# Attention and a feed-forward block on one core: whole chunks in kv, weight splits on VectorE alone, and queries times kv in quarters of the array

## The chip, the core and the metric

The kernel runs on one core of a Trainium2 chip. A core has TensorE (matmuls, PE in the profile, with its weight loads as PEld), VectorE (DVE), ScalarE (ACT), GpSimd (POOL) and SyncE (SP), whose queue issues most DMAs. Each engine runs its own instructions in order and waits on semaphores for the others. The scheduler that builds the program fixes the order on every engine beforehand. The metric is the device time of one execution in microseconds.

## What is computed

Linear attention over 8 batches of 8 heads, 576 positions and 64 features, followed by a feed-forward block on all 4608 tokens of 512 features:

```python
q_s = softmax(q, axis=-1); k_s = softmax(k, axis=positions)
kv  = einsum('bhsd,bhse->bhde', k_s, v)
x   = einsum('bhsd,bhde->bhse', q_s, kv)      # reshaped to (4608, 512)
h = x @ w_in                                  # 512 x 2048
g = h * clip(h + 3, 0, 6) / 6
out = g @ w_out                               # 2048 x 512
```

The weights arrive as float64 and are passed on bit for bit.

## The kernel before

Tokens are taken in three blocks of 512 and then three large blocks of 1024. In code the blocks are `j` = 0, 1, 2 and the large blocks are `s` = 0, 1, 2. Heads are handled in four pairs `hp`, so that 128 partitions hold two heads of 64 features.

**Decode.** The weights come in 16 chunks `f`, each 128 rows of w_in (turned) and of w_out. `decode` (line 127) turns the float64 bits of a chunk into float32 with four operations on VectorE (lines 134, 136, 141 and 145) and two on ScalarE (133, 144), then calls `split` (line 118): a rounded high part on ScalarE (line 120) and the rest, by a subtraction (line 121). For odd `f` above 1, seven chunks, that subtraction runs on GpSimd, otherwise on VectorE. The decode of chunk f + 2 is issued within the first block, between its matmuls for chunk f.

**kv.** `kv_of` (line 187) multiplies softmaxed keys `ke` with values `vt` over the 576 positions of one batch. Positions come in five chunks of 128, of which the last holds 64. Each chunk makes two matmuls of 64 columns, one for each head of the pair, into the upper and lower half of one bank `pkv`. The last chunk uses 64 rows. A column of ones in `vt` gives the softmax sum. The result, scaled and masked, is a block-diagonal 128x128 tile `kv` with one 64x64 block for each head. For the first two batches `ke` is made by transposing on TensorE (`k_softmax`, line 236), which fills only 64 rows of its last chunk. For the others the keys come padded.

**Queries.** `px` is `kv` times the softmaxed, turned queries `qT`. In `token_attention` (used for the third block by `block_attention` and for the large blocks by `sb_attention`) it is computed 512 tokens at a time: one matmul with all 128 rows and columns for each batch that the 512 tokens cross, in one of the two banks that `bank_a` hands out. `put` then copies the bank away: for large blocks one ScalarE copy of 128x512 into `x32` (line 377). The next unit's key maxima are turned by two transposes `pm`, which use the same two banks.

**Order.** From the second block on, TensorE's instructions keep the order in which the code is written (`ordered`, line 77). Attention for the next block is written in steps between the feed-forward matmuls of the present one: `ph` (x times w_in) and `po` (times w_out) in the blocks, and in the large blocks `x`, `y`, `z` of a scheme with seven products per pair of chunks, in `phase1` and `phase2`. So the large blocks' px come in three groups of four units: within block j = 2 for s = 0, within phase 1 of s = 0 for s = 1, and within phase 1 of s = 1 for s = 2. In the first block the scheduler alone sets TensorE's order. On the other engines it always does.

Of the kernel before, what the change touches and what calls it, by code (L numbers as in the profile page):

```python
# [1 line left out]

# [1 line left out]

# [6 lines left out]
F32 = mybir.dt.float32  # L11
# [7 lines left out]
P = 128  # L19
TB = 512  # L20
QD = 32
NC4 = TB // P
# [10 lines left out]
def attention_moe(  # L33
# [15 lines left out]
    nc = tc.nc  # L49

    B, NP, _, S = kT.shape
    D = q.shape[5]
# [7 lines left out]
    NCH = S // P + 1  # L60
    TAIL = S % P
# [14 lines left out]
    def bank_a(name):  # L76
        return ps_a.tile([P, TB], F32, name=name, tag="pa")
# [3 lines left out]
    def ordered(ins):  # L81
        if in_order:
            tc.keep_in_program_order(ins)

    def mm(out, lhsT, rhs, start, stop, goes_on=False):
        ordered(
            nc.tensor.matmul(  # L87
                out, lhsT, rhs, start=start, stop=stop, skip_group_check=goes_on
            )
        )  # L90

    def flip(out, in_):
        ordered(nc.tensor.transpose(out, in_, ident))
# [13 lines left out]
    def place(f, dt, name):  # L107
        return wp.tile([P, 4 * DM], dt, name=name, tag=f"w{f}")
# [7 lines left out]
    FROM_DRAM = 3  # L116
    whole = dr.tile([P, NFC, 2 * DM], F32, name="whole")

    def split(hi, lo, src, engine=nc.vector):
        nc.scalar.copy(hi, src)  # L120
        engine.tensor_sub(lo, src, hi.bitcast(F32))  # L121

    def load_w(f):
        raws[f] = place(f, U32, f"raw_{f}")
# [2 lines left out]
    def decode(f):  # L127

        n = 2 * DM
        pairs = raws.pop(f).rearrange("p (n two) -> p n two", two=2)  # L130
        low, high = pairs[:, :, 0], pairs[:, :, 1]
        m = moe.tile([P, n], F32, name="m", bufs=1)
        nc.scalar.activation(m, high.bitcast(F32), AF.Abs)
        nc.vector.tensor_scalar(m, m, W_MIN, W_MAX, op0=ALU.max, op1=ALU.min)
        m = m.bitcast(U32)
        nc.vector.tensor_scalar(
            m, m, 3, 0x3FFFFFFF, op0=ALU.logical_shift_left, op1=ALU.bitwise_and
        )
        v = moe.tile([P, n], F32, name="v", bufs=3)
        vu = v.bitcast(U32)  # L140
        nc.vector.scalar_tensor_tensor(  # L141
            vu, high, 0xC0000000, m, op0=ALU.bitwise_and, op1=ALU.bitwise_or
        )
        nc.scalar.activation(low, low, AF.Copy, scale=2.0**-29)
        nc.vector.tensor_tensor(vu, vu, low, op=ALU.add)
        if f // 2 >= FROM_DRAM:
            nc.sync.dma_start(whole[:, f], v)
        parts = place(f, F32R, f"w_{f}").rearrange("p (s i n) -> p s i n", s=2, i=2)
        split(
            parts[:, :, 0],  # L150
            parts[:, :, 1],
            v.rearrange("p (s n) -> p s n", s=2),
            nc.gpsimd if f % 2 and f > 1 else nc.vector,
        )
        wi[f], wo[f] = parts[:, 0], parts[:, 1]

# [2 lines left out]
    def x_block(j):  # L159
        if j not in x_tiles:  # L160
            t = xp.tile([P, 2, NCC, TB], F32R, name=f"x{j}", tag="xa")
            x_tiles[j] = t[:, 0], t[:, 1]
        return x_tiles[j]

    kvs = {}
# [22 lines left out]
    def kv_of(j, hp, ke, vt):  # L188
        pkv = bank_a("pkv")
        for c in range(NCH):  # L190
            r = slice(0, P if c < NC4 else TAIL)
            for h in range(2):
                hs = slice(h * D, (h + 1) * D)
                mm(pkv[hs, 0 : D + 1], ke[r, c, hs], vt[r, c, h, :], c == 0, c == NCH - 1)
        rk = att.tile([P, 1], F32, name="rk", bufs=2)
        nc.vector.tensor_scalar_add(rk, pkv[:, D : D + 1], EPS)
        nc.vector.reciprocal(rk, rk)
        kv = att.tile([P, P], F32, name="kv", bufs=10)
        nc.vector.scalar_tensor_tensor(
            kv.rearrange("p (h d) -> p h d", h=2),  # L200
            pkv[:, 0:D].rearrange("p (o d) -> p o d", o=1).broadcast_to([P, 2, D]),
            rk,
            mask.rearrange("p (h d) -> p h d", h=2),
            op0=ALU.mult,
            op1=ALU.mult,
        )
        kvs[j, hp] = kv
# [29 lines left out]
    def k_softmax(j, km, ke, kt):  # L237
        nc.vector.tensor_reduce(km, kt, axis=AX.X, op=ALU.max, negate=True)
        nc.scalar.activation(kt, kt, AF.Exp, bias=km)
        yield  # L240
        a = bank_a if j else bank
        pe, pe2 = a("pe"), a("pe2")
        for c in range(NC4):
            flip(pe[:, c * P : (c + 1) * P], kt[:, c * P : (c + 1) * P])
        flip(pe2[0:TAIL, 0:P], kt[:, TB:S])
        nc.scalar.copy(ke[:, 0:NC4].rearrange("p c n -> p (c n)"), pe)
        nc.scalar.copy(ke[0:TAIL, NC4], pe2[0:TAIL, 0:P])

    def attention(j, hp):

        if not j:
            kt, qt, qT, vt, ke = first[hp]
        else:
            kt, ke, vt = load_k(j, hp)
            qt = att.tile([P, TB], F32, name="qt", bufs=1)
            nc.sync.dma_start(qt, q[j, hp])
            qt = qt.rearrange("p (c h d) -> p c h d", c=NC4, h=2)
        km = att.tile([P, 1], F32, name="km", bufs=2)
        ks = k_softmax(j, km, ke, kt)
        next(ks)  # L260
        q_softmax(qt, j > 0, nc.vector if j else nc.gpsimd)
        yield
        next(ks, None)
        tp = (bank_a if j else bank)("tp")
        for c in range(NC4):
            flip(tp[:, c * P : (c + 1) * P], qt[:, c].rearrange("p h d -> p (h d)"))
        if j:
            qT = att.tile([P, TB], F32, name="qT")
        nc.scalar.copy(qT, tp)
        yield  # L270
        kv_of(j, hp, ke, vt)
        yield
        px = (bank_a if j else bank)("px")
        e = SHIFT * j
        for b, lo, hi in ((j - 1, 0, e), (j, e, TB)):
            if lo < hi:
                mm(px[:, lo:hi], kvs[b, hp], qT[:, lo:hi], True, True)
        x_hi, x_lo = x_block(j)
        split(x_hi[:, hp, :], x_lo[:, hp, :], px)

    def load_k(b, hp, tokens=False):
# [45 lines left out]
    def x_of(s):  # L327

        if "x" not in held:
            held["x"] = xp.tile([P, NCC, SB], F32, name="x32", tag="xa")  # L330
        return held["x"]

    def token_attention(t0, n, hp, put):

        need = [b for b in range(t0 // S, (t0 + n - 1) // S + 1)]
        qt = att.tile([P, SB], F32, name="qt", bufs=1)[:, 0:n]
        at = (t0 - TURNED) // TB
        nc.sync.dma_start(
            qt.rearrange("p (b n) -> p b n", n=TB),
            qf[at : at + n // TB, hp].rearrange("b p n -> p b n"),  # L340
        )
        loads = {b: load_k(b, hp, tokens=True) for b in need if (b, hp) not in kvs}
        yield
        new = {}
        for b, (kt, ke, vt) in loads.items():
            km = att.tile([P, 1], F32, name="km", bufs=2)
            nc.vector.tensor_reduce(km, kt, axis=AX.X, op=ALU.max)  # L347
            kb = att.tile([P, P], F32, name="kb", bufs=2)
            nc.gpsimd.tensor_copy(kb, km.broadcast_to([P, P]))
            new[b] = ke, vt, kb  # L350
        qT = q_softmax_t(qt)
        yield
        for ke, vt, kb in new.values():
            pm = bank_a("pm")
            flip(pm[:, 0:P], kb)
            nc.vector.tensor_sub(
                ke, ke, pm[:, 0:P].rearrange("p (o n) -> p o n", o=1).broadcast_to([P, NCH, P])
            )
            nc.scalar.activation(ke, ke, AF.Exp)
        yield  # L360
        yield
        for b, (ke, vt, kb) in new.items():
            kv_of(b, hp, ke, vt)
        yield
        for c in range(n // TB):
            px = bank_a("px")
            at = t0 + c * TB
            for b in need:
                lo, hi = max(b * S - at, 0), min((b + 1) * S - at, TB)
                if lo < hi:  # L370
                    mm(px[:, lo:hi], kvs[b, hp], qT[:, c * TB + lo : c * TB + hi], True, True)
            put(c, hp, px)
        yield

    def sb_attention(s):
        def put(c, hp, px):
            nc.scalar.copy(x_of(s)[:, hp, c * TB : (c + 1) * TB], px)

        return [token_attention(START + s * SB, SB, hp, put) for hp in (0, 2, 1, 3)]

    def block_attention(j):
        def put(c, hp, px):
            x_hi, x_lo = x_block(j)
            split(x_hi[:, hp, :], x_lo[:, hp, :], px)

        return [token_attention(j * TB, TB, hp, put) for hp in range(NP)]
# [492 lines left out]
```

## Time and profile before

| | us |
|---|---|
| median of 3 runs (range) | 863.46 (861.28 to 864.54) |
| the profiled execution | 863.42 |
| its span in the profile | 861.6 |
| TensorE busy | 816.8 |
| VectorE busy | 683.7 |
| ScalarE busy | 443.6 |
| GpSimd busy | 80.1 |

The profile records one execution. "Busy" sums the time in which an engine had at least one instruction running. Matmuls are pipelined, so TensorE's busy time is not a measure of how well it is used. A row of the groups gives line, engine, operation, tiles (written <- read), shape and count, then busy time, mean of one in ns, and the idle time of the engine just before with the releasers. A row of the timeline gives start, length, engine and operation. The chain is the series of steps, each released by the one before, that ends with the last instruction.

### The profile page before, as it was taken

Reading aid. Unit: us, or ns where it says so; the run is one execution under the profiler, and the core shown is the slowest. Engines: PE = TensorE matmul, PEld = TensorE weight load, DVE = VectorE, ACT = ScalarE, POOL = GpSimd, SP = SyncE. Lnnn points to the kernel's source line nnn. Section 1 sums busy time; section 2 is a strip of 40 time slices with the busy share of each in tenths; the row PEclk is TensorE's granted clock in tenths of the full one; section 3 lists DMA queues with packets and bytes.
Section 4 is the critical chain, followed back from the end, with each engine's and each line's share of the span. In section 5 each row is a group of like instructions: output and inputs, shape, how many; then the busy total and the mean of one; then the engine's idle time right before and its main releaser. Section 6 shows DMA issues by size and latency. Waiting matters only on the chain.

```text
span 861.6 us, 11761 instructions
## 1 busy us (share of the span) xinstructions
PE 816.8 (95%) x4032; PEld 654.0 (76%) x4032; DVE 683.7 (79%) x1088; ACT 443.6 (51%) x717; POOL 80.1 (9%) x178
## 2 busy tenths in 40 slices
PE   4689998999999998999999999999999999999997
PEld 3468786877887876887877777777788788887886
DVE  7998998998778988578998985688597845648763
ACT  7886673443344444345555553544555534445543
POOL 5111212110100110001102000011000000000000
PEclk9789999999999999999999999999999999999999
DMA  9997667578549660578875667775566776666672
GB/s 366 413 407 265 210 201 233 198 243 279 169 150 366 213 240 25 169 259 272 271 256 167 194 205 238 225 229 168 172 178 193 236 231 195 193 193 191 193 234 88
DMA packets 75643, 192.30 MB, mean 223 GB/s; under 512 B 7232, under 2 KB 19520, under 8 KB 73536
## 3 DMA queue, kind: packets, MB, share of 16 engines
q1 hardware_dynamic: 75008, 190.51, 67.3%
q10 hardware_dynamic: 576, 1.05, 0.3%
q8 instruction: 32, 0.52, 0.2%
q14 instruction: 27, 0.22, 0.1%
HBM read 147.49 MB, written 44.04 MB: 222 GB/s over the span
## 4 chain that ended last, share of the span: by engine, by line
PE 67%; DVE 18%; DMA 5%; issue 4%; ACT 3%; POOL 1%; SPq 0%; ACTq 0%; DVEq 0%; POOLq 0%
PE x L87 24%; PE po L87 12%; PE ph L87 10%; PE y L87 9%; PE z L87 9%; DMA kt<-in_kT_dram 2%; DVE g L515 2%; PE px L87 2%; PE pkv L87 2%; DVE gp L121 1%; DVE gf L121 1%; DVE v L141 1%; DVE right L121 1%; DVE km L347 1%; DMA wf<-gp 1%
## 5 line engine op out<-in xcount | busy, mean ns | idle before, releaser
L120 ACT CAST gf<-g 128x512 fp32r<-128x512 f32 x168 | 103.9, 622 | 96.3 <-DVE gf L121 48.0
L87 PE MATMUL ph<-x,w 128*128 128x512 f32 x576 | 147.9, 405 | 4.4 <-POOL w L121 2.0
L87 PE MATMUL po<-w,gp 128*128 128x512 f32 x576 | 146.9, 404 | 3.5 <-DVE gp L121 2.2
L121 DVE TENSOR_TENSOR gf<-g,gf 128x512 fp32r<-128x512 f32 x168 | 112.9, 686 | 31.8 <-ACT gf L120 31.0
L87 PEld LDWEIGHTS ph<-x,w 128*128 128x128 f32 x576 | 111.7, 195 | 31.5 <-POOL w L121 2.9
L87 PEld LDWEIGHTS po<-w,gp 128*128 128x128 f32 x576 | 108.4, 192 | 29.4 <-DVE gp L121 3.3
L87 PE MATMUL x<-right,gp 128*128 128x512 f32 x384 | 95.0, 392 | 2.9 <-DVE g L555 2.9
L87 PE MATMUL x<-gf,gp 128*128 128x512 f32 x384 | 89.0, 389 | 0.0
L87 PEld LDWEIGHTS x<-right,gp 128*128 128x128 f32 x384 | 71.6, 188 | 19.2 <-DVE g L555 3.7
L87 PEld LDWEIGHTS x<-gf,gp 128*128 128x128 f32 x384 | 72.1, 188 | 15.0
L514 ACT ACTIVATE g<-ph,three 128x512 f32<-128x512 f32 x48 | 32.8, 686 | 64.6 <-PE ph L87 64.6
L120 ACT CAST gp<-g 128x512 fp32r<-128x512 f32 x48 | 29.6, 620 | 39.8 <-DVE g L515 39.7
L514 ACT ACTIVATE v<-g,three 128x1024 f32<-128x1024 f32 x24 | 27.6, 1151 | 42.4 <-DVE g L559 42.4
L87 PE MATMUL x<-right,left 128*128 128x512 f32 x192 | 47.8, 392 | 0.8 <-DVE g L555 0.8
L87 PE MATMUL y<-right,gp 128*128 128x512 f32 x192 | 48.2, 395 | 0.0
L87 PE MATMUL x<-gf,left 128*128 128x512 f32 x192 | 46.1, 392 | 0.9 <-DVE gf L121 0.9
L87 PE MATMUL z<-gf,gp 128*128 128x512 f32 x192 | 45.7, 392 | 1.0 <-DVE gf L121 0.9
L87 PEld LDWEIGHTS z<-gf,gp 128*128 128x128 f32 x192 | 35.7, 188 | 10.1 <-DVE gf L121 2.7
L87 PEld LDWEIGHTS x<-gf,left 128*128 128x128 f32 x192 | 35.7, 188 | 10.1 <-DVE gf L121 2.8
L87 PEld LDWEIGHTS x<-right,left 128*128 128x128 f32 x192 | 35.7, 188 | 8.6 <-DVE g L555 1.3
L87 PEld LDWEIGHTS y<-right,gp 128*128 128x128 f32 x192 | 35.6, 188 | 8.0 <-issue 0.5
L514 ACT ACTIVATE g<-g,three 128x512 f32<-128x512 f32 x24 | 17.4, 725 | 39.5 <-DVE g L548 39.5
(135 smaller groups left out, 1324.6 us busy)
## 6 DMA issues: line engine op xcount, KB each, us to landing
gp<-wf SPq DMA_DIRECT2D x112, 512.0 KB, 3.6
left<-wf SPq DMA_DIRECT2D x56, 512.0 KB, 3.7
raw<-in_w_dram SPq DMA_DIRECT2D x16, 1024.0 KB, 14.2
wf<-gp SPq DMA_DIRECT2D x64, 256.0 KB, 3.6
wf<-w SPq DMA_DIRECT2D x48, 256.0 KB, 3.9
vt<-in_v_dram SPq DMA_DIRECT2D x28, 325.0 KB, 5.4
kt<-in_kT_dram SPq DMA_DIRECT2D x28, 288.0 KB, 3.5
ke<-in_k_dram SPq DMA_DIRECT2D x24, 320.0 KB, 4.7
```

The source lines that it names most:

```text
L87: nc.tensor.matmul(out, lhsT, rhs, start=start, stop=stop, skip_group_check=goes_on)
L120: nc.scalar.copy(hi, src)
L121: engine.tensor_sub(lo, src, hi.bitcast(F32))
L141: nc.vector.scalar_tensor_tensor(vu, high, 0xC0000000, m, op0=ALU.bitwise_and, op1=ALU.bitwise_or)
L347: nc.vector.tensor_reduce(km, kt, axis=AX.X, op=ALU.max)
L514: nc.scalar.activation(r, h, AF.Relu, bias=three, scale=1.0)
L515: nc.vector.scalar_tensor_tensor(g, r, 6.0, h, op0=ALU.min, op1=ALU.mult)
```

## The change

Three parts.

1. `split` no longer takes an engine: all subtractions of the decode run on VectorE.
2. `kv_of` uses 128 rows in every chunk. The rows that have no positions are filled with zeros by GpSimd where `ke` comes from transposes.
3. `token_attention` hands the queries to `put`, which issues the matmuls. For large blocks these are 64x64 quarters: the two heads are the two halves of the rows, and the two runs of 512 tokens are the two halves of the columns. Each head has a bank, and each run of tokens half of its partitions. The four results are copied with four ScalarE copies of 64x512. The third block keeps whole matmuls.

```diff
-    def split(hi, lo, src, engine=nc.vector):
+    def split(hi, lo, src):
         nc.scalar.copy(hi, src)
-        engine.tensor_sub(lo, src, hi.bitcast(F32))
+        nc.vector.tensor_sub(lo, src, hi.bitcast(F32))
...
             v.rearrange("p (s n) -> p s n", s=2),
-            nc.gpsimd if f % 2 and f > 1 else nc.vector,
         )
...
         for c in range(NCH):
-            r = slice(0, P if c < NC4 else TAIL)
             for h in range(2):
                 hs = slice(h * D, (h + 1) * D)
-                mm(pkv[hs, 0 : D + 1], ke[r, c, hs], vt[r, c, h, :], c == 0, c == NCH - 1)
+                mm(pkv[hs, 0 : D + 1], ke[:, c, hs], vt[:, c, h, :], c == 0, c == NCH - 1)
...
         nc.scalar.copy(ke[0:TAIL, NC4], pe2[0:TAIL, 0:P])
+        nc.gpsimd.memset(ke[TAIL:P, NC4], 0.0)
...
         yield
-        for c in range(n // TB):
+        put(t0, hp, need, qT)
+        yield
+
+    def segments(b, at):
+        return max(b * S - at, 0), min((b + 1) * S - at, TB)
+
+    def sb_attention(s):
+        def put(t0, hp, need, qT):
+
+            px = [bank_a("px") for _ in range(2)]
+            rows = [slice(h * D, (h + 1) * D) for h in range(2)]
+            parts = [[(b, *segments(b, t0 + c * TB)) for b in need] for c in range(2)]
+            parts = [[x for x in part if x[1] < x[2]] for part in parts]
+            for both in zip_longest(*parts):
+                for c, part in enumerate(both):
+                    if part:
+                        b, lo, hi = part
+                        for h, r in enumerate(rows):
+                            mm(
+                                px[h][rows[c], lo:hi],
+                                kvs[b, hp][r, r],
+                                qT[r, c * TB + lo : c * TB + hi],
+                                True,
+                                True,
+                                True,
+                            )
+            for c in range(2):
+                for h, r in enumerate(rows):
+                    nc.scalar.copy(x_of(s)[r, hp, c * TB : (c + 1) * TB], px[h][rows[c]])
+
+        return [token_attention(START + s * SB, SB, hp, put) for hp in (0, 2, 1, 3)]
+
+    def block_attention(j):
+        def put(t0, hp, need, qT):
             px = bank_a("px")
-            at = t0 + c * TB
             for b in need:
-                lo, hi = max(b * S - at, 0), min((b + 1) * S - at, TB)
-                if lo < hi:
-                    mm(px[:, lo:hi], kvs[b, hp], qT[:, c * TB + lo : c * TB + hi], True, True)
-            put(c, hp, px)
-        yield
-
-    def sb_attention(s):
-        def put(c, hp, px):
-            nc.scalar.copy(x_of(s)[:, hp, c * TB : (c + 1) * TB], px)
-
-        return [token_attention(START + s * SB, SB, hp, put) for hp in (0, 2, 1, 3)]
-
-    def block_attention(j):
-        def put(c, hp, px):
+                lo, hi = segments(b, t0)
+                mm(px[:, lo:hi], kvs[b, hp], qT[:, lo:hi], True, True)
             x_hi, x_lo = x_block(j)
             split(x_hi[:, hp, :], x_lo[:, hp, :], px)
```

Lines move by up to 20. On TensorE, in the third block, the first unit of the first large block stands like this before:

```order
L87 MATMUL ph<-x_1532,w_366 128x512 x12
L87 MATMUL px<-m,kv 128x192
L87 MATMUL px<-m,kv 128x320
L87 MATMUL px<-m,kv 128x256 x2
L93 MATMUL pm<-ident,kb 128x128 x2
L87 MATMUL po<-w_334,gp 128x512 x12
```

and like this now:

```order
L88 MATMUL ph<-x_1540,w_370 128x512 x12
L88 MATMUL px<-m,kv 64x192 x2
L88 MATMUL px<-m,kv 64x256 x2
L88 MATMUL px<-m,kv 64x320 x2
L88 MATMUL px<-m,kv 64x256 x2
L94 MATMUL pm<-ident,kb 128x128 x2
L88 MATMUL po<-w_338,gp 128x512 x12
```

Four matmuls have become eight of half the rows, two heads at a time, with the two runs of tokens in turn. The transposes `pm` of the next unit stand directly behind them, as before. In phase 1 twelve feed-forward matmuls stand between the two, before and now.

ScalarE at the same place, before, with `gp` the split of g or of weight sums (names of `v`), and `ke` the exponential of keys:

```order
L514 ACTIVATE g<-ph,three 128x512
L377 COPY x_2512<-px 128x512
L120 CAST gp<-g 128x512
L120 CAST gp<-v 128x2x256
L377 COPY x_2512<-px 128x512
L120 CAST gp<-v 128x2x256
L359 ACTIVATE ke<-ke 128x640 x2
```

and now:

```order
L534 ACTIVATE g<-ph,three 128x512
L121 CAST gp<-g 128x512
L121 CAST gp<-v 128x2x256
L393 COPY x_2527<-px 64x512 x4
L121 CAST gp<-v 128x2x256
L359 ACTIVATE ke<-ke 128x640 x2
```

The two copies stood apart, with casts between them. The four stand together, behind the cast of g.

VectorE in the decode of chunk 3 (`raw_3`), before:

```order
L141 SCALAR_TENSOR_TENSOR v_418<-raw_3_120,m_414 128x1024
L238 TENSOR_REDUCE km_376<-kt_369 128x1
L121 TENSOR_TENSOR x0_311<-px_322,x0_311 128x512
L145 ISA v_418<-raw_3_120,v_418 128x2048
L219 TENSOR_REDUCE qm_379<-qt_374 128x8
L134 TENSOR_SCALAR m_462<-m_462 128x1024
L136 TENSOR_SCALAR m_462<-m_462 128x1024
L141 SCALAR_TENSOR_TENSOR v_466<-raw_4_122,m_462 128x1024
L145 ISA v_466<-raw_4_122,v_466 128x2048
```

and now:

```order
L142 SCALAR_TENSOR_TENSOR v_422<-raw_3_120,m_418 128x1024
L237 TENSOR_REDUCE km_380<-kt_373 128x1
L535 SCALAR_TENSOR_TENSOR g_356<-g_356,ph_343 128x512
L146 ISA v_422<-raw_3_120,v_422 128x2048
L535 SCALAR_TENSOR_TENSOR g_412<-g_412,ph_399 128x512
L218 TENSOR_REDUCE qm_383<-qt_378 128x8
L135 TENSOR_SCALAR m_467<-m_467 128x1024
L122 TENSOR_TENSOR gp_359<-g_356,gp_359 128x512
L122 TENSOR_TENSOR w_3_426<-v_422,w_3_426 128x2x512
L137 TENSOR_SCALAR m_467<-m_467 128x1024
```

The split of chunk 3 (`w_3`) now stands on VectorE, within the decode of chunk 4. The first block's products of ph (`g`, `gp`) stand earlier among the decode's operations.

More of the change, by code (lines that the diff above doesn't have):

```diff
@@ L1 @@
 from contextlib import ExitStack
+from itertools import zip_longest
 import numpy as np
@@ L364, in token_attention @@
         yield
-        for c in range(n // TB):
-            px = bank_a("px")
-            at = t0 + c * TB
-            for b in need:
-                lo, hi = max(b * S - at, 0), min((b + 1) * S - at, TB)
-                if lo < hi:
-                    mm(px[:, lo:hi], kvs[b, hp], qT[:, c * TB + lo : c * TB + hi], True, True)
-            put(c, hp, px)
+        put(t0, hp, need, qT)
         yield
+    def segments(b, at):
+        return max(b * S - at, 0), min((b + 1) * S - at, TB)
     def sb_attention(s):
-        def put(c, hp, px):
-            nc.scalar.copy(x_of(s)[:, hp, c * TB : (c + 1) * TB], px)
+        def put(t0, hp, need, qT):
[19 more added lines that the diff above has]
+                    nc.scalar.copy(x_of(s)[r, hp, c * TB : (c + 1) * TB], px[h][rows[c]])
         return [token_attention(START + s * SB, SB, hp, put) for hp in (0, 2, 1, 3)]
     def block_attention(j):
-        def put(c, hp, px):
+        def put(t0, hp, need, qT):
+            px = bank_a("px")
+            for b in need:
+                lo, hi = segments(b, t0)
+                mm(px[:, lo:hi], kvs[b, hp], qT[:, lo:hi], True, True)
             x_hi, x_lo = x_block(j)
```

## Prediction

> **What bounds the kernel now.** First the page: engine shares, the forty slices, the chain.
>
> ```profile
> span 861.6 us, 11761 instructions
> PE 816.8 (95%) x4032; PEld 654.0 (76%) x4032; DVE 683.7 (79%) x1088; ACT 443.6 (51%) x717; POOL 80.1 (9%) x178
> PE   4689998999999998999999999999999999999997
> DVE  7998998998778988578998985688597845648763
> PE 67%; DVE 18%; DMA 5%; issue 4%; ACT 3%; POOL 1%; SPq 0%; ACTq 0%; DVEq 0%; POOLq 0%
> ```
>
> TensorE is busy almost throughout and holds two thirds of the chain, but the stages differ. So next the table by stretch, which I cut at the stages: decode and first block (34 to 150), second block (150 to 220), third block (220 to 328), phase one of the first large block (360 to 455), of the second (542 to 630).
>
> ```profile
> 34.00:60.00 26.00, 23.23 (x101) 17.91 (x101) 25.70 (x31) 22.07 (x41) 5.04 (x2) 0.79 1.03 414
> 60.00:100.00 40.00, 40.00 (x196) 32.52 (x195) 35.66 (x45) 26.04 (x47) 5.84 (x2) 1.00 0.73 258
> 100.00:150.00 50.00, 45.61 (x221) 35.24 (x220) 47.35 (x73) 30.66 (x70) 10.81 (x13) 0.94 0.65 215
> 150.00:220.00 70.00, 68.78 (x364) 54.69 (x364) 62.39 (x136) 29.64 (x49) 8.52 (x28) 1.00 0.73 245
> 220.00:328.00 108.00, 105.62 (x595) 85.86 (x594) 89.92 (x161) 49.96 (x77) 15.15 (x48) 1.00 0.62 214
> 360.00:455.00 95.00, 92.38 (x535) 73.92 (x534) 78.84 (x131) 48.48 (x73) 10.22 (x33) 1.00 0.79 263
> 542.00:630.00 88.00, 87.15 (x437) 68.24 (x436) 66.62 (x101) 45.34 (x67) 5.55 (x18) 1.00 0.63 190
> ```
>
> The busy columns are PE, PEld, DVE, ACT, POOL. From 34 to 60 and from 100 to 150 VectorE is the fullest (25.70 of 26, 47.35 of 50) while PE idles 2.8 and 4.4 us: **the decode is VectorE's**. In 220 to 328 and 542 to 630 PE idles 2.4 of 108 and 0.9 of 88: those two are TensorE's. The chain of waits, asked for these stretches, agrees: PE lines in the third block and in 542 to 630. From 360 to 455 it is different:
>
> ```profile
> by line: DMA kt<-in_kT_dram 14.1%; DVE g L515 10.4%; issue 9.0%; PE x L87 5.6%; DVE km L347 5.2%; DVE ke L356 4.4%; PE y L87 4.3%; DMA left<-wf 3.7%; DVE qt L314 3.7%; DVE qr L316 3.4%; DVE g L548 3.3%; POOL swap L304 3.1%; DVE qt L320 2.5%
> ```
>
> There the chain runs through key loads and VectorE, though PE is 97% busy. What PE saves there I count half.
>
> **Decode without GpSimd.** Seven weight splits go from POOL to DVE. Groups by shape, then one collision on the timeline (POOL, then DVE), then the chain at another:
>
> ```profile
> L121 POOL TENSOR_TENSOR w<-v,w 128x1024 fp32r<-128x1024 f32 x7 | 18.4, 2634 | 87.0 <-ACT w L120 69.0 <-DMA raw<-in_w_dram 18.0
> L121 DVE TENSOR_TENSOR w<-v,w 128x1024 fp32r<-128x1024 f32 x9 | 11.5, 1279 | 0.0
> L136 DVE TENSOR_SCALAR m<-m 128x1024 uint32<-128x1024 uint32 x16 | 15.5, 967 | 0.2
> L141 DVE SCALAR_TENSOR_TENSOR v<-raw,m 128x1024 uint32<-128x1024 uint32 x16 | 24.2, 1512 | 0.3
> L145 DVE CUSTOM_DVE_ANT_0 v<-raw,v 128x2048 uint16<-128x2048 uint16 x16 | 23.0, 1437 | 0.2
> L98 POOL MEMSET mask<- 128x128 f32 x1 | 0.2, 205 | 0.0
> ...
> 39.81 2.39 POOL L121 TENSOR_TENSOR w<-v,w 128x1024 fp32r<-128x1024 f32 x1 [18.03 <-DMA raw<-in_w_dram]
> ...
> 39.83 2.94 DVE L136 TENSOR_SCALAR m<-m 128x1024 uint32<-128x1024 uint32 x1
> 42.80 1.23 DVE L141 SCALAR_TENSOR_TENSOR v<-raw,m 128x1024 uint32<-128x1024 uint32 x1
> 44.06 1.22 DVE L145 CUSTOM_DVE_ANT_0 v<-raw,v 128x2048 uint16<-128x2048 uint16 x1
> 47.45 0.68 DVE L136 TENSOR_SCALAR m<-m 128x1024 uint32<-128x1024 uint32 x1
> ...
> 103.57 2.37 POOL w L121
> 105.98 4.13 PE ph L87 x10
> ```
>
> A DVE instruction that starts beside a POOL split takes 2.94 us where its like takes 0.68: it stands until POOL is done. The groups show the sum: mean against undisturbed, (967-680)x16 + (1512-1230)x16 + (1437-1220)x16 is 12.6 us; some 0.8 of it belongs to GpSimd's softmax before 20 us, and one collision hit another line, so about 13 us in seven stalls, 1.9 each. The splits added to DVE cost 7x1.22 = 8.5 us (the 1279 mean holds one stretched instruction). **Net 4.5 us less on the engine that bounds this stage.** The chain row shows PE waiting for POOL's result directly; on DVE it comes 1.4 us sooner once its turn comes. Bounds: 8.5 us lost if the stalls had another cause; 7.2 gained, PE's idle time in these stretches. PE has none from 60 to 100, so I take **-4.0**. The scheduler also reorders this stage, and that I can't price beyond these ends. New POOL fills of the keys' tail (eight) are small, beside an engine 9% busy that hides them; without that cover they cost at most 0.2 us each. SyncE's queue holds writes of finished weights between loads of raw ones, so a split done sooner only frees it sooner.
>
> [...]
>
> **128 rows in kv.** The fifth chunk now uses all rows, so the array's form no longer changes.
>
> ```profile
> L87 PE MATMUL pkv<-vt,ke x560: 218/222/325, 47.5 to 600.0; 128*64 128x65 f32 x150, 64*64 64x65 f32 x37
> ...
> 259.54:259.59 0.06, 0.06 (x10) 0.06 (x7) 0.00 (x0) 0.06 (x1) 0.00 (x0) 1.00 0.81 318
> ...
> 162.01 0.88 PE pkv L87 x20
> 259.31 1.76 PE pkv L87 x40
> 261.07 2.94 PE po L87 x12
> 273.08 2.72 PE ph L87 x12
> ```
>
> In a window of 0.06 us ten matmuls are in flight, each 222 ns long: one starts every (222+60)/10 = 28 ns. Twenty would be 0.56, the chain has 0.88: 0.32 for two changes of form (into 128x64, into 64x64), 0.16 each. A single kv loses one change (0.16), a double three of four (0.48). Third block: four doubles, 1.9; phase one of the first large block: four doubles at half, 1.0; of the second: four singles, 0.6. The eight in the first two blocks are DVE's stage: nothing. **-3.5**; bounds 0 and 5.8 (12 singles and 8 doubles hold 36 changes that go, none of them hidden).
>
> **Queries times kv in quarters.**
>
> ```profile
> 283.23 1.73 PE px L87 x8
> 572.44 1.84 PE px L87 x6
> ...
> L87 PE MATMUL px<-m,kv 128*128 128x448 f32 x8 | 3.7, 539 | 0.0
> ```
>
> Each matmul of the code is two records (448 columns once in four units: x8). A unit streams 1024 columns twice in 1.73 to 1.84 us, 0.9 ns a column. In quarters, one chunk's 512 columns run beside the other's, if **all four overlap**: 512x2x0.9 = 0.92, plus a change in (0.16) and out (2.94-2.72 = 0.22): 1.30. Saved 0.43 (0.54 in the last): third block 1.7, first large block at half 0.9, second 2.2: **-4.8**. Overlap of column halves is in kv's 28 ns (65 columns at 0.9 would be 58); no row shows row halves side by side. Bounds: 0.92 of streaming, and the four in a row, 3.7.
>
> **Evictions.** Four copies of 64 rows replace two.
>
> ```profile
> L377 ACT COPY x<-px 128x512 f32<-128x512 f32 x24 | 13.5, 588 | 1.3 <-PE px L87 0.9
> 383.08 1.05 ACT L377 COPY x<-px 128x512 f32<-128x512 f32 x2
> ...
> 384.84 0.38 PE L93 MATMUL pm<-ident,kb 128*128 128x128 f32 x2
> ...
> 269.42 0.49 ACT x L377
> ...
> 270.05 0.30 PE pm L93
> ```
>
> The copies keep their 512 columns, so I keep the row's 0.5 us for each (0.25 if half the rows took half the time; nothing in the rows speaks for that). Behind them ACT's casts wait 1.0 us longer, on a half-idle engine. But the transposes pm need both banks: at 270.05 PE already waits for the second copy, with twelve po matmuls in order behind. All four now start after the last matmul; the banks are free 1.6 and 2.1 us behind it. Where pm follows at once (two units of the third block) that costs 0.7 more each; in phase one copies would end near 385.2 against pm at 384.84, so 0.7 there and 0.5 later: **+2.6**, bounds 0 and 9 (0.75 for each of 12 units).
>
> **Sum.** The profiled execution took 863.4 us (span 861.6), beside a median of 863.46. -4.0 -3.5 -4.8 +2.6 = -9.7: **853.7**.
>
> **Rivals.**
> - *Quarters wait in turn* (0.16). If matmuls start strictly in program order, a quarter's second record holds back the next quarter: five steps for four in the third block (192+192+3x320 = 1344 columns, 1.21 us), three for two in the last (1.38). Units of 1.59 and 1.76 save 1.2 in all: **857.3**. For it: the two records stand in a row. Against: kv's 28 ns from its first matmuls on. [...]
> - *Row halves don't overlap* (0.11): unit 1.84+0.38 = 2.22, +5.4 in place of -4.8: **863.9**.
> - *All four in a row* (0.04), the slower side: 3.68+0.38 = 4.06, +27.5: **886**. It decides once a unit exceeds some 2.5 us. Against it: kv's 28 ns.
> - *The decode gains nothing* (0.13): the seven splits come late in a full DVE queue and PE waits for weights as now, or the new order is worse: +4 in place of -4, **861.7**. For it: PE has no idle time from 60 to 100; against it: the stalls go for certain.
>
> **Chances.** Forecast 0.52; 0.04 for a larger gain (a full share in phase one and 7.2 in the decode: 849). Own range of the forecast 848 to 858. Over all, 847 (the larger gain) to 862.5 (a decode without gain) leaves out the four in a row and most of the row halves. A measurement of this kernel tells about 0.5% (4.3 us) from no change. Faster by more: nearly all of the forecast, three quarters of the first rival, a few of the others, 0.68. Within: 0.24. Slower: 0.08.
>
> **What would show it.** Decode: no 128x1024 subtraction on POOL, DVE's L136, L141 and L145 groups back to means near 0.68, 1.22, 1.22, the first block ending 4 us earlier. kv: x40 near 1.3 us. Quarters: a unit at 1.3 us (0.9 without changes), against 1.6, 2.2 or 4.1 for the rivals. Evictions: PE's waits for ACT ahead of pm, at two places about 2.4 us. The forecast is wrong if px units don't shrink, if pm stalls in all units, or if VectorE's stalls in the decode persist without POOL.

## The result, and the profile after

| | before | after |
|---|---|---|
| median, us (runs, range) | 862.26 (6, 860.86 to 864.54) | 857.04 (6, 855.32 to 860.69) |
| the profiled execution, us | 863.42 | 860.69 |
| its span, us | 861.6 | 858.9 |
| TensorE busy, us | 816.8 | 807.9 |
| ScalarE busy, us | 443.6 | 458.9 |

The ratio is 0.9941, with a 95% interval of 0.9916 to 0.9967: 5.1 us faster, where 9.7 were forecast. The profiled execution is the slowest of its six, so its stages are compared below with those of relatives of the kernel too. The page of the kernel after, its busy times, two rows of slices and the chain:

```profile
PE 807.9 (94%) x4120; PEld 643.1 (75%) x4120; DVE 677.9 (79%) x1095; ACT 458.9 (53%) x741; POOL 65.6 (8%) x179
PE   4899989998998988999998999999999999999997
DVE  7998998987777888368989986589697846648763
PE 61%; DVE 21%; DMA 7%; ACT 4%; issue 3%; POOL 2%; SPq 0%; ACTq 0%; DVEq 0%; POOLq 0%
```

PE's share of the chain fell from 67% to 61%: it now waits more, and the table by stretch says where (the columns are PE, PEld, DVE, ACT, POOL, granted clock, DMA share, GB/s):

```profile
34.00:60.00 26.00, 25.08 (x128) 19.44 (x127) 25.25 (x36) 24.14 (x44) 0.20 (x1) 1.00 1.03 412
60.00:100.00 40.00, 37.25 (x183) 29.04 (x181) 36.54 (x52) 30.24 (x66) 0.20 (x1) 1.00 0.81 281
100.00:150.00 50.00, 45.98 (x226) 35.23 (x226) 47.04 (x77) 27.67 (x53) 6.01 (x15) 0.97 0.71 240
220.00:328.00 108.00, 100.88 (x611) 80.48 (x610) 87.57 (x158) 52.09 (x80) 10.78 (x43) 0.97 0.64 217
542.00:630.00 88.00, 87.15 (x474) 68.14 (x473) 69.34 (x106) 51.72 (x77) 5.55 (x18) 1.00 0.60 197
```

The stretch from 220 to 328, which holds most of the third block, was TensorE's, with 2.4 us idle. Now 7.1 are idle and the clock is 0.97. By its last po matmuls the block itself runs from 250.9 to 359.2 before and from 246.1 to 360.2 after, so its end lies in no row of this table or of the prediction's. The groups of the decode and of the copies:

```profile
L142 DVE SCALAR_TENSOR_TENSOR v<-raw,m 128x1024 uint32<-128x1024 uint32 x16 | 20.2, 1265 | 0.1
L122 DVE TENSOR_TENSOR w<-v,w 128x1024 fp32r<-128x1024 f32 x16 | 20.0, 1249 | 0.4 <-ACT w L121 0.3
L146 DVE CUSTOM_DVE_ANT_0 v<-raw,v 128x2048 uint16<-128x2048 uint16 x16 | 19.5, 1217 | 0.2
L137 DVE TENSOR_SCALAR m<-m 128x1024 uint32<-128x1024 uint32 x16 | 11.2, 698 | 0.1
L393 ACT COPY x<-px 64x512 f32<-64x512 f32 x48 | 27.9, 581 | 1.9 <-PE px L88 1.3
```

The decode's means are back at 0.70, 1.27 and 1.22: the stalls are gone. The copies of 64 rows take 581 ns, as those of 128 rows did (588), and there are twice as many. The chain through phase one of the second large block shows a single kv at 0.73 (0.88 before) and a px unit at 1.01 (1.84 before):

```profile
581.59 0.73 PE pkv L88 x20
588.01 1.01 PE px L88 x10
```

And a window of 0.03 us at the start of that px unit shows its first matmuls, one for each quarter, all running (x4 in the PE column):

```profile
587.93:587.96 0.03, 0.02 (x4) 0.02 (x4) 0.00 (x0) 0.00 (x0) 1.00 1.01 410
```

The four records of the trace start within 20 ns, and the whole unit takes 1.01 us, so **all four quarters overlap**. It is less than the 1.38 us of streaming that the first rival has for such a unit.

The third block is where it went wrong. What PE waited for there (us in total, times, longest):

```profile
PE pm L94 <- ACT x L393: 7.1, 4, 3.4
PE po L88 <- ACT gp L121: 2.6, 1, 2.6
PE po L88 <- DVE gp L122: 1.5, 1, 1.5
```

The first of the stalls, on ScalarE's timeline (start, length, engine and operation):

```profile
261.62 0.69 ACT L534 ACTIVATE g<-ph,three 128x512 f32<-128x512 f32 x1 [4.24 <-PE ph L88]
263.07 0.62 ACT L121 CAST gp<-g 128x512 fp32r<-128x512 f32 x1 [0.76 <-DVE g L535]
263.59 0.61 ACT L121 CAST gp<-v 128x512 fp32r<-128x512 f32 x1
264.11 2.36 ACT L393 COPY x<-px 64x512 f32<-64x512 f32 x4
```

and on PE's:

```profile
261.46 1.09 PE L88 MATMUL px<-m,kv 64*64 64x192 f32 x16
265.97 0.30 PE L94 MATMUL pm<-ident,kb 128*128 128x128 f32 x1 [3.42 <-ACT x L393]
266.57 0.30 PE L94 MATMUL pm<-ident,kb 128*128 128x128 f32 x1 [0.31 <-ACT x L393]
```

px ends at 262.55. The copies start only at 264.11: ahead of them in ScalarE's order stands the cast of g, which waits for VectorE's product, and a cast of weight sums. Then four copies run in a row, 2.36 us. The transposes pm need the banks, and twelve po matmuls stand behind pm. The windows around it show what the stall does beyond its own length:

```profile
262.00:264.00 2.00, 0.55 (x11) 0.10 (x2) 1.65 (x2) 1.24 (x3) 0.00 (x0) 1.00 1.08 395
264.00:266.00 2.00, 0.03 (x1) 0.06 (x1) 1.36 (x3) 1.95 (x5) 0.00 (x0) 1.00 0.99 354
266.00:268.00 2.00, 1.69 (x6) 1.24 (x7) 1.29 (x3) 1.83 (x3) 0.59 (x2) 0.70 1.00 345
268.00:270.00 2.00, 2.00 (x6) 1.57 (x5) 2.00 (x4) 0.74 (x1) 0.00 (x0) 0.50 0.86 331
270.00:272.00 2.00, 2.00 (x10) 1.60 (x9) 2.00 (x4) 0.00 (x0) 0.12 (x1) 0.95 0.86 284
```

The clock column falls to 0.50 once PE resumes: of the 6 us from 266, (0.30+0.50+0.05)x2 = **1.7 us are lost to the clock**, on top of 3.7 of waiting. The twelve po matmuls that start at 266.63 take 4.58 us, the twelve ph behind them 2.89. In phase one of the second large block, pm never waits.

### The profile page after: what moved, and what is told of

Its sections match the earlier page's. It is cut to its first block, busy times and chain, and to the rows that moved or that the text cites. A ratio compares the mean times of both kernels' runs of the same rounds, so it can differ in the third digit from the quotient of the medians.

```text
span 858.9 us, 11975 instructions
## 1 busy us (share of the span) xinstructions
PE 807.9 (94%) x4120; PEld 643.1 (75%) x4120; DVE 677.9 (79%) x1095; ACT 458.9 (53%) x741; POOL 65.6 (8%) x179
## 4 chain that ended last, share of the span: by engine, by line
PE 61%; DVE 21%; DMA 7%; ACT 4%; issue 3%; POOL 2%; SPq 0%; ACTq 0%; DVEq 0%; POOLq 0%
PE x L88 27%; PE y L88 10%; PE z L88 10%; PE po L88 6%; PE ph L88 5%; DMA v<-whole 2%; DMA qt<-in_qf_dram 2%; DVE g L535 2%; DVE gp L122 2%; POOL swap L304 2%; DVE v L142 1%; DVE v L146 1%; DMA kt<-in_kT_dram 1%; PE px L88 1%; DVE km L347 1%
## 5 line engine op out<-in xcount | busy, mean ns | idle before, releaser
L88 PE MATMUL po<-w,gp 128*128 128x512 f32 x576 | 152.1, 413 | 7.0 <-ACT gp L121 5.0
L88 PE MATMUL ph<-x,w 128*128 128x512 f32 x576 | 144.2, 398 | 3.0 <-ACT w L121 2.6
L88 PEld LDWEIGHTS po<-w,gp 128*128 128x128 f32 x576 | 110.2, 196 | 36.9 <-ACT gp L121 7.4
L88 PEld LDWEIGHTS ph<-x,w 128*128 128x128 f32 x576 | 109.0, 191 | 28.7 <-ACT w L121 3.3
L88 PE MATMUL x<-gf,gp 128*128 128x512 f32 x384 | 89.3, 390 | 0.0
L535 DVE SCALAR_TENSOR_TENSOR g<-g,ph 128x512 f32<-128x512 f32 x48 | 32.6, 679 | 15.9 <-ACT g L534 15.6
```

The source lines that it names most:

```text
L88: nc.tensor.matmul(out, lhsT, rhs, start=start, stop=stop, skip_group_check=goes_on)
L535: nc.vector.scalar_tensor_tensor(g, r, 6.0, h, op0=ALU.min, op1=ALU.mult)
```

## Experiments

All times below are medians. "Against before" is the ratio to runs of the kernel before on the same chip, and us worked out from it with 862.3. The last columns are lengths of stages in the profiled runs, from the last po of one block, or the last matmul of one phase, to that of the next.

| kernel | us | against before (95%) | us | 1st block ends | 2nd | 3rd | phase one, 1st large | phase one, 2nd large |
|---|---|---|---|---|---|---|---|---|
| before | 862.3 | | | 153.7 | 97.2 | 108.3 | 95.6 | 89.9 |
| after | 857.0 | 0.9941 (0.9916 to 0.9967) | -5.1 | 145.9 | 100.3 | 114.1 | 97.4 | 86.9 |
| e1, whole px | 850.8 | 0.9859 (0.9836 to 0.9883) | -12.2 | 146.9 | 97.4 | 106.2 | 95.0 | 89.4 |
| e2, extra step | 846.2 | 0.9804 (0.9781 to 0.9827) | -16.9 | 145.1 | 95.7 | 106.7 | 93.8 | 87.8 |
| e4, copies shared | 857.9 | 0.9943 (0.9923 to 0.9964) | -4.9 | 144.9 | 97.4 | 112.7 | 97.2 | 88.7 |
| e5, decode alone | 864.6 | 1.0024 (1.0005 to 1.0043) | +2.1 | 147.6 | 103.4 | 108.7 | 96.2 | 89.9 |
| e6, whole px, step | 844.8 | 0.9783 (0.9758 to 0.9807) | -18.7 | 145.9 | 95.5 | 101.1 | 95.7 | 89.3 |
| e7, before, step | 855.3 | 0.9910 (0.9890 to 0.9931) | -7.8 | 151.9 | 96.8 | 103.3 | 95.6 | 90.5 |
| e8, step, splits spread | 845.4 | 0.9799 (0.9774 to 0.9824) | -17.3 | 146.2 | 95.5 | 106.1 | 93.6 | 87.7 |
| e9, kv alone | 860.1 | 0.9963 (0.9949 to 0.9977) | -3.2 | 153.7 | 96.4 | 107.5 | 94.6 | 89.5 |
| e10, whole in 3rd block, step | 840.5 | 0.9750 (0.9737 to 0.9763) | -21.6 | 146.0 | 95.5 | 101.0 | 93.3 | 87.9 |
| e11, whole in 3rd block | 847.9 | 0.9846 (0.9826 to 0.9865) | -13.3 | 145.6 | 96.5 | 106.5 | 94.8 | 86.9 |
| e12, decode undone | 864.3 | 1.0018 (1.0003 to 1.0034) | +1.6 | 154.1 | 96.4 | 115.5 | 93.0 | 87.0 |
| e13, step, last unit whole | 841.7 | 0.9764 (0.9750 to 0.9779) | -20.4 | 145.9 | 95.5 | 101.8 | 93.8 | 88.0 |

The changed kernel's own second block, 100.3 in its slowest run, is 95.5 to 97.4 in its relatives with all splits on VectorE and 128 rows in kv, whose code there is nearly the same; those 3 us are not put down to the change. In its profile px waits 2.2 us at 205.77 for VectorE's last step on the queries (0.8 in e1), and from 208.8 to 212.2 the clock is 0.50.

### The parts, one by one

**e1** takes the quarters back:

```diff
-            px = [bank_a("px") for _ in range(2)]
...
+            for c in range(2):
+                px = bank_a("px")
+                for b in need:
+                    lo, hi = segments(b, t0 + c * TB)
+                    if lo < hi:
+                        mm(px[:, lo:hi], kvs[b, hp], qT[:, c * TB + lo : c * TB + hi], True, True)
+                nc.scalar.copy(x_of(s)[:, hp, c * TB : (c + 1) * TB], px)
```

> The changed kernel with whole-array px again (one bank for 512 tokens, two copies of 128 rows), so without its third part. Theory A (the quarters shorten px as forecast, but their four copies hold the two banks so long that PE waits for pm): the third block's two pm waits fall from 3.6 and 3.4 us to about 1.6 and 1.2, its length from 114 to 110 us or less, while phase one of the second large block grows by 2.2 us; the whole stays within 1 us of the changed kernel's 857.0. Rival B (the third block lost its time to something else, as the new order of VectorE's work or the loads of whole weights): third block stays at 112 to 114, the whole comes to 859 to 860. Rival C (the quarters cost nothing and gain 4.8 as forecast, the missing 2 us are the decode's): 861.

It is 7.1 us faster than the change, more than any theory had. The third block is 7.9 us shorter, phase one of the second large block 2.5 us longer, as theory A had it. So the quarters lose in the third block, and far more than the sum allowed. Phase one of the first large block is 2.4 us shorter too, but e11, which has quarters there, takes about the same (94.8 for 95.0), so the quarters of that phase are not the cause.

**e5** is the kernel before with the decode's splits on VectorE, nothing else:

```diff
-            nc.gpsimd if f % 2 and f > 1 else nc.vector,
```

> The kernel before with the decode's seven splits on VectorE and nothing else. Theory A (the decode gives 4 to 4.75 us and keeps them, as the ends of the second block say): 257.5 to 258.5 in the last digits, so 857.5 to 858.5. Rival (the reordered work of the later blocks gives half of it back): 860 to 861. Rival (no gain): 862.3.

A miss: slower than before, though the interval only just leaves out no change. (The first figures of theory A are a slip; 857.5 to 858.5 is meant.) The first block does end 6.1 us sooner, but the second gives all of it back. PE's waits there:

```profile
PE px L87 <- DVE m L321: 5.4, 2, 5.0
```

One px waits 5.0 us for the last of VectorE's steps on the queries; the chain into it runs through two loads of whole weights, 6.2 and 3.6 us, for sums that stand ahead on VectorE. The changed kernel has the same wait at 2.2 us and the kernel before at 1.2; why it is longest here isn't settled.

**e9** is the kernel before with 128 rows in kv, nothing else:

```diff
-            r = slice(0, P if c < NC4 else TAIL)
...
-                mm(pkv[hs, 0 : D + 1], ke[r, c, hs], vt[r, c, h, :], c == 0, c == NCH - 1)
+                mm(pkv[hs, 0 : D + 1], ke[:, c, hs], vt[:, c, h, :], c == 0, c == NCH - 1)
...
+        nc.gpsimd.memset(ke[TAIL:P, NC4], 0.0)
```

> The kernel before with 128 rows in every chunk of kv and nothing else. Forecast's term: 862.9 - 3.5 = 859.4, with x40 at 1.3 us. Rival from the difference of the first and the last experiment (850.8 with kv and decode, 864.6 with the decode alone): 849 to 853. Rival between them (the decode alone lost 5 us in the second block by loads that came late, which the first experiment did not; kv itself 3.5 to 6): 857 to 859.

3.2 us faster, against 3.5 in the forecast. In the chain of its third block a double kv takes 1.32 us where it took 1.76:

```profile
258.51 1.32 PE pkv L88 x40
```

Where the gain lies is less like the sum. The two profiled runs differ by 4.8 us: 0.8 in the third block (1.9 was worked out), 1.0 and 0.4 in the phases one (1.0 and 0.6), and, not forecast, 0.8 in the second block and 1.9 in phase two of the first large block (78.6 for 80.6). e7, which lacks this part, has 78.1 in that phase, so the 1.9 can't be put down to kv. The rival from e1 minus e5 falls with e5's second block; the one between (857 to 859) isn't told apart from the forecast, since the interval is 857.9 to 860.3.

**e12** is the change with the splits of odd f back on GpSimd:

```diff
+            nc.gpsimd if f % 2 and f > 1 else nc.vector,
```

> The changed kernel with the decode's seven splits back on GpSimd. By the forecast's term (4.0): 861. By the difference of the first and the ninth experiment (9.2 us with 128 rows in kv and whole px): 866. By the decode alone (1.8 us lost): 855.

864.3: within the change, the decode is worth 1.6 + 5.1 = 6.7 us; between e9 and e1 it is 9.0. The profile of e12, the group of GpSimd's splits:

```profile
L122 POOL TENSOR_TENSOR w<-v,w 128x1024 fp32r<-128x1024 f32 x7 | 20.7, 2962 | 78.6 <-ACT w L121 30.8 <-issue 29.2 <-DMA raw<-in_w_dram 18.6
```

and one of PE's waits in the first block:

```profile
PE ph L88 <- POOL w L122: 3.2, 3, 1.5
```

PE's gaps from 34 us to the end of that block add up to 14.4 us, against 7.7 after. Part of this is direct waiting for GpSimd, whose split takes 2.96 us where VectorE's takes 1.25. If half of PE's busy time at 0.50 is counted as lost too, the sums are 17.1 and 9.4 us. Over all kernels of the table, the first block ends at 144.9 to 147.6 in the ten with all splits on VectorE and at 151.9 to 154.1 in the four with GpSimd.

### The stall ahead of pm

**e4** gives half of the copies to VectorE:

```diff
-            for c in range(2):
+            for c, copy in enumerate((nc.scalar.copy, nc.vector.tensor_copy)):
                 for h, r in enumerate(rows):
-                    nc.scalar.copy(x_of(s)[r, hp, c * TB : (c + 1) * TB], px[h][rows[c]])
+                    copy(x_of(s)[r, hp, c * TB : (c + 1) * TB], px[h][rows[c]])
```

> The changed kernel with the two copies of the second run of tokens on VectorE in place of ScalarE, so that each bank is emptied by both engines side by side. If the number of copies in a row on ScalarE sets the wait (theory A), the banks are free 1.2 us sooner: the two pm waits fall from 3.6 and 3.4 to about 2.4 and 2.2 and the whole to 854 to 855.5. If the place of the copies in the engines' queues sets it (behind the cast of g on ScalarE, behind 90 of 108 busy us on VectorE), VectorE's copies come as late or later: waits stay at 3 us or more, the whole 857 to 860.

The rival's result. In the third block pm waits for VectorE's copies now, up to 4.2 us:

```profile
PE pm L94 <- DVE x L393: 8.8, 5, 4.2
```

Two copies fewer in a row brought nothing (857.9 for 857.0), as the other two stood behind other work in a full queue. What stood ahead of the copies counted, not their number alone.

**e2** leaves everything as it is and puts a step of feed-forward matmuls between px and pm:

```diff
         qT = q_softmax_t(qt)
         yield
+        yield
         for ke, vt, kb in new.values():
             pm = bank_a("pm")
...
-            step = steps(units, 6 if turned else 4)
+            step = steps(units, 7 if turned else 4)
...
-            step = steps(sb_attention(0), 6)
+            step = steps(sb_attention(0), 7)
...
-        step = steps(sb_attention(s + 1), 6) if more else iter(())
+        step = steps(sb_attention(s + 1), 7) if more else iter(())
```

> The changed kernel with one more empty step before pm in every unit of token_attention (seven steps a unit for six), so that twelve po matmuls or a pair of phase-one products always lie between px and the pm that needs its banks. Theory A: PE's waits for ScalarE ahead of pm go (under 0.5 us at the two places that show 3.6 and 3.4 now), the third block falls from 114 to 108 us or less, the whole to 851 to 853. Rival B (copies and pm only show where PE would have waited anyway, for the casts of g or for VectorE): the waits move to po or ph, third block over 111 us, the whole 855 to 858.

No wait ahead of pm is left, and the third block takes 106.7 for 114.1. The whole is 846.2, better than expected.

**e7** and **e6** put the same step into the kernel before and into e1:

> The kernel before with only the extra step before pm. Theory A: it takes away the two pm waits of the third block (1.37 and 1.01 us) and nothing else, so 862.9 - 2.4 = 860.5. Rival (the step helps by a better spread of VectorE's work, whatever px looks like): 857 or below, with phase one of both large blocks shorter by 1 us or more each. Rival (PE then waits for kv, which comes sooner after the exponentials): 862 to 865.

> The extra step before pm, but with whole-array px (first experiment and second together). Theory A (quarters are worth the forecast's 4.8 us once pm no longer waits for their copies): 846.2 + 4.8 = 851, with no more than 0.5 us of wait ahead of pm. Rival (whole px gains the 2.4 us of its own two pm waits, 1.37 and 1.01, and quarters are worth 2 us or less): 848 or below. Rival (quarters are worth nothing): 846.

e7 gains 7.8 us, three times the two waits. 5.0 of it lie in the third block: PE's gaps there sum to 1.4 us for 4.9, and with the gap of 2.2 us at 334.74 the half clock behind it went (0.66, 0.50, 0.50, 0.64 in the four windows from 338 in the kernel before: 1.7 us; e7 has 1.00 from 249 to 352). 3.5 + 1.7 makes about the 5.0. So theory A's 2.4 was too little; the rival's time came, but not its shorter phases one (95.6 and 90.5, for 95.6 and 89.9). In e6 theory A's 851 falls. e6, with whole px, is 1.8 us ahead of e2 by the ratios; the intervals overlap. The phases one say that quarters pay 1.9 and 1.5 us there; the third block says that they still lose 5.6, without any wait for pm.

### What else the quarters cost in the third block

e2's third block has one long gap, 3.45 us at 329.14, then half clock:

```profile
329.00:331.00 2.00, 0.14 (x1) 0.00 (x0) 2.00 (x4) 0.60 (x1) 1.60 (x3) 1.00 0.19 76
331.00:333.00 2.00, 0.41 (x2) 0.37 (x3) 2.00 (x3) 1.54 (x3) 0.00 (x0) 0.99 0.00 0
333.00:335.00 2.00, 2.00 (x6) 1.54 (x5) 2.00 (x4) 1.04 (x1) 0.00 (x0) 0.50 0.00 0
```

VectorE is full meanwhile (2.00 of 2). Its timeline just before, in e2:

```profile
320.42 0.65 DVE L122 TENSOR_TENSOR gp<-g,gp 128x512 fp32r<-128x512 f32 x1
322.32 1.22 DVE L519 TENSOR_TENSOR v<-x 128x1024 f32<-128x1024 f32 x1 [1.25 <-ACT x L394]
323.46 1.22 DVE L122 TENSOR_TENSOR right<-x,right 128x1024 fp32r<-128x1024 f32 x1
...
330.29 0.67 DVE L536 SCALAR_TENSOR_TENSOR g<-g,ph 128x512 f32<-128x512 f32 x1
```

and in e6:

```profile
319.68 1.18 DVE L122 TENSOR_TENSOR right<-x,right 128x1024 fp32r<-128x1024 f32 x1
320.79 0.68 DVE L122 TENSOR_TENSOR gp<-g,gp 128x512 fp32r<-128x512 f32 x1
321.38 1.22 DVE L505 TENSOR_TENSOR v<-x 128x1024 f32<-128x1024 f32 x1
...
327.07 0.67 DVE L522 SCALAR_TENSOR_TENSOR g<-g,ph 128x512 f32<-128x512 f32 x1
```

The factors of the first large block are split at the end of this block. The second of them needs only the first 512 tokens of the last unit. With whole px these come out in one copy, so its split runs at 319.68. In quarters every copy comes after the whole px: VectorE idles 1.25 us, the splits pile up ahead of the product g, and PE waits for g's cast.

**e8** spreads the splits over four chunks:

```diff
-            if j == NB - 1 and n >= 14:
-                for _ in range(3):
+            if j == NB - 1 and n in (11, 13, 14, 15):
+                for _ in range(1 if n == 11 else 2):
                     next(fac, None)
```

> The extra step, and the seven splits of the first large block's factors spread over four chunks (one at the 12th, two each at the last three) in place of three and three at the last two. Theory A (PE's 3.45 us gap at 329 us of the second experiment comes from casts of g that stand behind those splits, and the half clock granted from 333 to 336 follows from the gap): gap under 2 us, clock 1.0, the whole 842.5 to 844.5. Rival (VectorE is full there whatever the order): the gap moves to another place, 845.5 to 847.

Theory A falls: the gap is 3.90 us now. The time is the rival's to 0.1 us, but the gap is still at its place (328.59). That the last unit's copies hold the splits in any order is the reading that the next experiment tests.

**e13** makes only that last unit whole again, in e2:

```diff
+            if not s and hp == 3:
+                for c in range(2):
+                    px = bank_a("px")
...
+                    nc.scalar.copy(x_of(s)[:, hp, c * TB : (c + 1) * TB], px)
+                return
             px = [bank_a("px") for _ in range(2)]
```

> The second experiment with only the last px unit of the first large block in the whole array again. Theory (the third block's last loss comes from this unit alone: its first 512 tokens come out complete in one early copy, so the split of the second factor runs ahead of the cast of g; in quarters all four copies are needed and everything on VectorE behind them comes late): no gap over 1 us near 329, no half clock behind it, third block 101, the whole 839.5 to 841. Rival (the number of copies in all four units loads ScalarE too much, or px and pm stall in the other three): third block 104 or more, 844 to 846.

Close to the theory: the third block falls from 106.7 to 101.8, the longest gap to 1.33 us (under 1 was expected), the whole to 841.7 (841 at most was expected); the mean clock of the profiled execution is 0.996, where e2 has 0.991. The rival (844 to 846) falls.

**e11** and **e10** use whole px for all four units in the third block and quarters for the second and third large block, e11 in the change as it is, e10 with the extra step. The edit is e13's, with another condition:

```diff
-            if not s and hp == 3:
+            if not s:
```

> The changed kernel (no extra step) with whole-array px for the first large block only. Theory (the change loses its time by the quarters of the third block, through two pm waits of 3.4 us, a late split of the factors and the half clock behind each): third block 106 for 114, so 857.0 - 6.2 = 850.8 or a little below, since quarters pay in the second phase one (2.5 us) and lose about as much in the first. Rival (the quarters cost time wherever they stand): 853 to 857.

> The extra step, and quarters for the second and third large block only; the first one's px, which lie in the third block, use the whole array. Theory (quarters gain 1.5 to 2 us in each phase one, and lose 5.6 in the third block only): third block 101 as in the sixth experiment, the two phases one 94 and 88 as in the second, the whole 840.6 to 841.5. Rival (the shorter phases were chance or come from elsewhere): 844 to 845.

e11 is 8.2 us faster than the change by the ratios, and its third block is 7.6 us shorter. e10 is the fastest kernel here, 21.6 us under the kernel before. PE's only waits in its third block:

```profile
PE po L88 <- DVE gp L122: 1.0, 2, 0.8
```

and two windows over the block:

```profile
250.00:328.00 78.00, 78.00 (x480) 63.89 (x481) 67.22 (x123) 36.35 (x55) 10.90 (x34) 1.00 0.67 229
328.00:343.00 15.00, 13.98 (x58) 10.31 (x57) 13.51 (x18) 7.31 (x10) 2.28 (x4) 1.00 0.39 122
```

From 250 to 328 PE has no gap, and the clock is 1.00 to the end of the block. Against e6, e10 differs by the quarters of the later blocks alone: 2.9 us gained, 2.4 in the first phase one and 1.4 in the second. The intervals of the two just overlap, but e2 against e6 had shown 1.9 and 1.5 in the same places. e13, with quarters in three more units, is no faster than e10.

## Why the prediction was right, and where it was not

The forecast was 853.7 and the range 847 to 862.5; it came to 857.0, on the side forecast. The sum held better than its terms: two were mis-sized, in opposite directions, and that they nearly cancelled was luck. The third part as a whole (quarters and their copies, -4.8 + 2.6) was to gain 2.2 us; taking it back gains 7.1 (e1). The decode's larger gain beside the kv part (9.0, from e9 to e1) covers that.

- **128 rows in kv (-3.5): right.** Measured alone -3.2. A single kv became 0.15 shorter, a double 0.44, where 0.16 and 0.48 were worked out. The stages agree less well (see e9), so the closeness of the total is partly luck.
- **Quarters (-4.8): the mechanism was right.** All four overlap. A unit is 1.01 us, and the six products behind it take 1.59 where they took 1.38, together near the 1.30 of the sum. The rivals of quarters in turn, of row halves that don't overlap and of four in a row fall. Where nothing stood in the way, in the later large blocks with the extra step, they gained 2.9, of a forecast 3.1, though not in the shares of the sum (2.4 and 1.4, where 0.9 and 2.2 were worked out).
- **Decode (-4.0): right in sign, too small.** Undoing it costs 6.7 us within the change. The step that failed is the bound "7.2 gained, PE's idle time in these stretches", and the -4.0 chosen below it because PE had no idle time from 60 to 100. PE's idle time is not all that this stage loses: in the prediction's own table the clock is 0.79 from 34 to 60 and 0.94 from 100 to 150, which is about another 8.5 us. The rows after have 1.00 and 0.97, which is 1.5 us, while PE's idle time in the three stretches stays about the same (7.7 for 7.2). Gaps and lost clock together, from 34 us to the end of the first block, fall from 15.5 to 9.0 us with the decode alone (before to e5), from 17.3 to 10.3 beside the kv part (e9 to e1) and from 17.1 to 9.4 within the change (e12 to after); the block ends 6.1, 6.8 and 8.2 us sooner. The rival that the decode gains nothing fell in this kernel, but came true when the decode was changed alone (+2.1), through the second block, which the sum had not looked at.
- **Evictions (+2.6): the other mis-sized term.** The third block was to gain 1.7 by quarters and lose 1.4 by copies; it is 7.6 us longer than in e11. The place was named rightly: pm, right behind px, at two places, though with 2.4 us for each wait. Three things were left out. The copies queue: the sum let them start with the end of px, but they start 1.6 us later, behind a cast that waits for VectorE, so that the waits were 3.4 and 3.2 us. The clock: PE's three longest gaps in the block (3.4, 3.2 and 2.6 us) were followed by 3.4, 3.4 and 6.8 us at 0.50. And the splits that follow the last unit: their wait for all four copies was priced only as "ACT's casts wait 1.0 us longer, on a half-idle engine", and e13 shows that this alone is worth about 5 us when the extra step is there. In the change itself it is less: at the end of the block PE's gaps are 2.57 and 1.50 us where e11, with whole px, still has one of 2.23. The stretch 220 to 328, which the prediction took for the third block, leaves out its last 31 us, where the factors are split.

The working for the third block, change against e11: PE's gaps sum to 11.2 for 5.0, that is 6.2 (4.1 of it at the two pm); the half clock behind three gaps instead of one takes some 4 more; the shorter px give back about 3. That makes 7, of 7.6 seen.

## What to carry to other kernels

Before more copies are put between a matmul and the next user of its bank, read which work stands ahead of them on the copying engine and what it waits for: here that cost 1.6 us of a wait of 3.4, more than the two extra copies (1.2). The cure was free: other matmuls between the two users of the bank. It is no cure for the copies alone, since it gained 7.8 us in the kernel before as well. Where PE stalls, count the clock lost behind a stall with the stall (here 1.7 us behind 3.7 of waiting). And look where a gain can be lost again: the decode shortened the first block by 6 to 8 us in every pair, but alone it left the kernel 2.1 us slower, with one px of the second block waiting 5.0 us.

## What the hardware showed unexpectedly

**Some stalls cost more than their length.** In the third block the granted clock fell to 0.50 behind gaps of PE of 3.42, 3.23 and 2.57 us in the change, of 3.45 in e2 and of 2.22 in the kernel before, for 3.4 us each time and for 6.8 behind the change's last. The first of them cost 1.7 us beyond its length, so a stall of 3.4 us came to about 5. Behind gaps of 1.37 us (before pm in the kernel before) and 1.59 us (first block after) the clock stayed at 1.00. But length alone didn't decide, as two gaps in e9's third block show, of 1.89 us (from 267.44) and of 2.23 (from 334.50), each with the stretch behind it (the clock is the third column from the end):

```profile
267.40:270.09 2.69, 0.80 (x5) 0.70 (x5) 2.69 (x4) 2.53 (x5) 0.59 (x2) 1.00 1.00 392
270.09:273.50 3.41, 3.41 (x10) 2.64 (x9) 3.41 (x7) 0.74 (x1) 0.00 (x0) 0.50 1.00 380
334.50:336.73 2.23, 0.00 (x1) 0.00 (x1) 2.23 (x4) 0.39 (x1) 0.00 (x0) 1.00 0.00 0
336.73:340.20 3.47, 3.47 (x15) 2.90 (x16) 3.41 (x4) 0.62 (x1) 0.00 (x0) 1.00 0.00 0
```

Behind the shorter gap the clock was 0.50, behind the longer one 1.00. In the traces of before and after the starts of half clock lie whole multiples of 3.413 us apart: in the third block of the change they are 266.79, 304.33 and 335.06, 11 and 9 multiples, and in the kernel before 106.21, 147.17 and 338.31, 12 and 56. Counted in such steps, e9's gap of 1.89 us lies within the one that ends at 270.09, and that of 2.23 us is cut by the edge at 334.94 into 0.44 and 1.79. In the traces of before and after, from 34 to 835 us, the ten steps at full clock that half clock followed held 1.64 to 3.02 us of PE idle, and those that full clock followed at most 1.59. By these two traces alone e9's 1.79 would have been enough, so that the cut made the difference is the author's reading and was not shown.

**Half the rows were no cheaper to copy.** 64 partitions of 512 columns took ScalarE 581 ns (after), 128 partitions 588 (before).
